# Pooled attention and a mixing block on one core: the softmax division moved behind the attention phase, and a new order of work inside it

## The chip, the cores and the metric

One core of one Trainium2 chip runs the whole program in one launch. The metric is the time of the device in microseconds (us), median of the runs. The engines are named as in the profile: PE (matrix multiply; PEld is its weight load), DVE (vector), ACT (scalar), POOL (GpSimd) and SP, whose queue issues nearly all DMAs.

## The reference

```python
# q, k, v: (8, 8, 1152, 64); the weights of the second part come in double precision (float64)
q_pool = q.reshape(B, H, S // 2, 2, D).mean(axis=3)
scores = scale * np.matmul(q_pool, k.transpose(0, 1, 3, 2))
scores = scores - np.max(scores, axis=-1, keepdims=True)
attn = np.exp(scores)
attn = attn / (np.sum(attn, axis=-1, keepdims=True) + 1e-09)
attn_out = np.matmul(attn, v)
x = attn_out.transpose(0, 2, 1, 3).reshape(B, 576, 512)

theta = x @ w_theta
zr, zi = x * np.cos(theta), x * np.sin(theta)
y = einsum('ts,bsd->btd', w_tok_r, zr) + einsum('ts,bsd->btd', w_tok_i, zi)
u = x + y
out = u + np.maximum(u @ w_ch, 0.0)
```

## The kernel before, in words

There are two phases. **Phase one** is the attention. It goes over 32 *pairs* (8 batches, 4 pairs of heads each; the two heads of a pair share the 128 partitions). Each pair has

- `prep`: PE transposes K and the pooled Q into a PSUM tile `pt` (`prep_t`, L240), in two groups; ACT rounds it to `hi` (`prep_hi`, L256), DVE takes the rest `lo` (`prep_lo`, L267), and ACT copies the last 64 queries of each head into `tail` (`prep_tail`, L263);
- the maxima: 12 products `pm` of Q blocks with K (`maxpass`, L280), each reduced by DVE (L287), and the `tail` products `px` and a corner of `pt` (`max_tail`, L297 and L303), reduced by DVE at L306 and L307. `max_nm` joins them to `nm`, `max_row` transposes `nm` on PE (L317) and ACT copies the row to `mT` (L319), and `load_max` spreads `mT` by four small DMAs into `nmr`, which the scores add as a fourth term;
- the scores, 18 units (u is the half of the queries, kt the block of keys): 8 matrix products `pe` (`escore`, L346), the exponential on ACT into `pc` (L349), and for 14 of the 18 a running sum `ss` on POOL (`ssum`, L358);
- `av`, twice: 36 recorded products `pa` of `pc` with V (L367), copied to `xu` by ACT (L374);
- the normalisation: `norm_sum` adds the sums over partitions on PE (L383), ACT adds epsilon into `sm` (L392). `norm_spread` writes `sm` to DRAM, `norm_load` reads it back over 128 partitions, DVE inverts it (L407), `norm_save` writes it, `norm_bcast` reads it with two DMAs as `dn` over all partitions, `norm_out` multiplies `xu` by `dn` on DVE (L429), and `norm_store` writes the result to `xd`.

The order is a table of positions. One unit of position is one score unit, so a pair is 18 long; `at(pos, ...)` collects every step, and all are emitted sorted by position. Every engine and SP's queue run in that order. `AV_AT` puts two *bursts* into a pair. Burst 0 (10.348) is `prep` group 1 of pair i+2, the maxima row of pair i+1, `av` 0, and `norm_sum` of pair i-1. Burst 1 (19.269) is `prep` group 0 of pair i+3, `max_tail` of pair i+2, and `av` 1. PSUM tiles of phase one (`bank2`) come from one ring of four double banks: whoever takes the next one waits until the user four places earlier is read out. K lies in one tile `kn`: its load for pair i+3 starts after burst 0 and must have landed for burst 1.

Between these steps lie the steps of `weights`, a generator that turns the double words of the weights into single precision and splits them (18 jobs: 8 square blocks, 10 token blocks). One call of it per position in `W_AT` does one step: a load, or one DVE, ACT or POOL operation (L500 to L530), or for a token block five transposes on PE (L565, L572) with their splits.

**Phase two** is the mixing block, one batch per 56 units of its own table (some 60 us): `xload` brings `xT` from `xd` into one of two buffers, ACT and the `xlo` engine split it (`xh` L700, `xl` L704), PE forms `theta` (`pth`, L724), `chain` makes sine and cosine factors on DVE and ACT and splits them, with the lower parts `Z` on POOL (L771), and PE multiplies them with the token weights (`py`, L796) and the channel weights (`pr`, L835).

Of the kernel before, what the change touches and what calls it, by code (L numbers as in the profile page):

```python
# [78 lines left out]
def pooled_attention_moe_kernel(  # L79
# [83 lines left out]
    with ExitStack() as p1:
# [128 lines left out]
        def max_tail(i, pt):  # L292
# [13 lines left out]
            nc.vector.tensor_reduce(mx[:, 8, 0:2], pm, AX.X, ALU.max)  # L306
# [7 lines left out]
        def max_row(i):  # L314
            st = state[i]
            px = bank2("e", f"pmt{i}")
            nc.tensor.transpose(out=px[0:KT, 0, 0:P], in_=st["nm"], identity=ident)  # L317
            mT = st["mT"] = sml.tile([KT, P], F32R, tag="mT", name=f"mT{i}")
            nc.scalar.copy(mT, px[0:KT, 0, 0:P])  # L319
            return px  # L320
# [39 lines left out]
        def av(i, u):  # L360
            st = state[i]
            if u == 0:
                st["xu"] = nrm.tile([P, 2, HALF], F32, tag="xu", name=f"xu{i}", bufs=3)
# [10 lines left out]
            nc.scalar.copy(st["xu"][:, u, :], pa[:, 0, 0:HALF])  # L374

# [18 lines left out]
        def norm_spread(i):  # L394
            st = state[i]
            rdi = st["rd"] = dram.tile([4, HALF], F32, tag="rd", name=f"rd{i}", bufs=2)
            nc.sync.dma_start(rdi, st["sm"].rearrange("(n r) c -> n r c", r=32)[:, 0, :])

        def norm_load(i):
            st = state[i]  # L400
            rc = st["rc"] = sml.tile([P, SQ * 2 // P], F32, tag="rc", name=f"rc{i}")
            rdv = st["rd"].rearrange("n c -> (n c)").rearrange("(p j) -> p j", p=P)
            nc.sync.dma_start(rc, rdv)

        def norm_recip(i):
            rc = state[i]["rc"]
            nc.vector.reciprocal(rc, rc)  # L407

        def norm_save(i):
            st = state[i]  # L410
            rdo = st["ro"] = dram.tile([4, HALF], F32, tag="ro", name=f"ro{i}", bufs=2)
# [4 lines left out]
        def norm_bcast(i):
            st = state[i]
            dn = st["dn"] = nrm.tile([P, 2, HALF], F32, tag="dn", name=f"dn{i}")
            for h in range(2):
                nc.sync.dma_start(  # L420
                    dn[h * D : (h + 1) * D].rearrange("a u c -> a (u c)"),
                    st["ro"].rearrange("(h u) c -> h (u c)", h=2)[h : h + 1, :].broadcast_to(
                        [D, SQ]
                    ),
                )

        def norm_out(i):
            st = state[i]
            nc.vector.tensor_tensor(st["xu"], st["xu"], st["dn"], ALU.mult)  # L429
# [33 lines left out]
        def norm_store(i):
# [5 lines left out]
            del state[i]  # L469

        def weights():
# [8 lines left out]
            def fetch(parts, n):  # L480
                ws = wst.tile([P, SQ], F32, tag="ws", name="ws")
                raw = wst.tile(
                    [P, SQ, 2 if wide else 1], U32 if wide else F32, tag="raw", name="raw"
# [3 lines left out]
                return raw, ws  # L487

            def narrow(raw, ws, R, n, g):
                dst = ws[0:R, 0:n].rearrange("a (t p) -> a p t", t=g)  # L490
                if not wide:
                    nc.vector.tensor_copy(
                        dst, raw[0:R, 0:n, 0].rearrange("a (p t) -> a p t", t=g)
                    )
                    return
# [7 lines left out]
                nc.vector.tensor_scalar(f, hi, 0x7FFFFFFF, None, ALU.bitwise_and)  # L503
# [455 lines left out]
```

## Time and profile before

| what | us |
|---|---|
| median of 3 runs (1422.18 to 1427.7) | 1422.18 |
| span of the profiled execution, first to last instruction | 1422.1 |
| start of `av` 0 of the first pair | 44.86 |
| start of `av` 0 of the 30th pair, 29 periods later | 857.53 |
| that stretch: PE busy / POOL busy | 768.15 / 697.91 |
| from 950 to 1400 (phase two in its stride): PE busy of 450 | 447.76 |

The profiled execution agrees with the median to 0.1 us, so nothing that matters lies around the span. "Busy" of PE includes waits inside a run of matrix products, since their ends are modelled. A row of the timeline reads: start, duration, engine, line and operation, what it writes from what, count, and in brackets how long the engine had been idle and what ended that. A row of the waits reads: who waited for whom, total time, how often, the longest. A row of the windows reads: stretch, its length, then busy time of PE, PEld, DVE, ACT and POOL with counts, the granted clock, the share of the DMA engines and GB/s. A row of the chain that ended last reads: start, duration, what.

### The profile page before, as it was taken

The page shows a single profiled execution, that of the slowest core. Times are in us where ns is not written, and L with a number is a line of the kernel's source. Part 1 is how long each engine was busy: PE and PEld are TensorE (multiplying, and loading weights), DVE is VectorE, ACT ScalarE, POOL GpSimd, SP SyncE. Part 2 cuts the span into 40 slices and gives each one's busy share as a digit, 9 for nine tenths or more (in the row PEclk, how much of TensorE's full clock was granted, in tenths as well). Part 3 has the DMA queues.
Part 4 walks back from the last instruction along what each step waited for, and adds up shares of the span by engine and source line. Part 5 has one row for each costly group of instructions (what it writes and reads, how often), then busy time and mean ns, then how long its engine had stood idle before and what let it go on. Part 6 is the DMA issues. An engine that isn't in the chain of part 4 may idle for free.

```text
span 1422.1 us, 29902 instructions
## 1 busy us (share of the span) xinstructions
PE 1343.2 (94%) x12178; PEld 1094.5 (77%) x12178; DVE 858.6 (60%) x1140; ACT 724.5 (51%) x1254; POOL 913.0 (64%) x671
## 2 busy tenths in 40 slices
PE   5999899999999999999998999989999999999998
PEld 4767677767766776767676776679999999999998
DVE  5866676667677767766675667165353543536342
ACT  2555455646555565556564655564344544445431
POOL 2789788988897998879987898842323313232210
PEclk9999999999999999999999999989999999999999
DMA  5224333424342353324333431321111111111111
GB/s 126 74 75 128 82 101 93 110 83 125 94 116 79 98 140 89 91 83 126 99 94 85 118 85 49 98 100 38 34 38 34 52 57 34 38 34 42 30 32 36
DMA packets 130906, 111.66 MB, mean 79 GB/s; under 512 B 95040, under 2 KB 95424, under 8 KB 130768
## 3 DMA queue, kind: packets, MB, share of 16 engines
q1 hardware_dynamic: 130592, 109.28, 28.0%
q8 instruction: 96, 1.57, 0.5%
q0 software_dynamic: 176, 0.46, 0.1%
q14 instruction: 42, 0.34, 0.1%
HBM read 88.29 MB, written 21.27 MB: 77 GB/s over the span
## 4 chain that ended last, share of the span: by engine, by line
PE 64%; DVE 18%; ACT 6%; DMA 5%; issue 3%; POOL 3%; SPq 1%; ACTq 0%; POOLq 0%; DVEq 0%
PE pe L346 15%; PE py L796 13%; PE pa L367 11%; PE pth L724 7%; DVE mx L287 6%; PE pr L835 6%; PE pm L280 3%; PE pt L240 3%; DMA kn<-in_k_dram 2%; PE pmt L383 2%; POOL ss L358 2%; DVE lo L267 2%; DVE ws L505 1%; DVE wf L503 1%; DVE mx L306 1%
## 5 line engine op out<-in xcount | busy, mean ns | idle before, releaser
L358 POOL TENSOR_TENSOR ss<-ss,pc 128x576 f32<-128x576 f32 x384 | 561.0, 1461 | 110.8 <-ACT pc L349 88.7
L287 DVE TENSOR_REDUCE mx<-pm 128x2 f32<-128x768 f32 x384 | 344.5, 952 | 138.2 <-PE pm L280 138.0
L349 ACT ACTIVATE pc<-pe 128x576 f32<-128x576 f32 x576 | 365.0, 652 | 90.0 <-PE pe L346 71.6
L367 PE MATMUL pa<-pc,vn 128*64 128x288 f32 x2304 | 293.5, 409 | 1.1 <-PE pmt L317 1.0
L771 POOL TENSOR_TENSOR Z<-ab,Z 128x512 fp32r<-128x512 f32 x40 | 52.3, 1308 | 315.1 <-ACT Z L767 315.1
L796 PE MATMUL py<-wtk,Z 128*128 128x288 f32 x1728 | 244.7, 299 | 6.9 <-DVE r L741 6.9
L367 PEld LDWEIGHTS pa<-pc,vn 128*64 128x64 f32 x2304 | 162.3, 137 | 109.5 <-ACT pc L349 3.2
L796 PEld LDWEIGHTS py<-wtk,Z 128*128 128x128 f32 x1728 | 235.7, 191 | 8.7 <-DVE r L741 7.5
L346 PE MATMUL pe<-hi 64*128 64x288 f32 x1152 | 206.4, 353 | 19.2 <-DVE lo L267 17.5
L346 PEld LDWEIGHTS pe<-hi 64*128 64x128 f32 x1152 | 110.6, 187 | 87.5 <-issue 28.8
L346 PE MATMUL pe<-lo,hi 64*128 64x288 f32 x1152 | 173.3, 296 | 0.0
L346 PE MATMUL pe<-hi,lo 64*128 64x288 f32 x1152 | 173.0, 295 | 0.0
L346 PE MATMUL pe<-nmr,oner 64*128 64x288 f32 x1152 | 172.3, 294 | 0.0
L280 PE MATMUL pm<-hi 64*128 64x384 f32 x768 | 138.2, 357 | 10.8 <-DVE mx L306 6.0
L256 ACT CAST hi<-pt 128x768 fp32r<-128x768 f32 x64 | 56.2, 878 | 117.8 <-DVE mx L307 103.1
L346 PEld LDWEIGHTS pe<-lo,hi 64*128 64x128 f32 x1152 | 112.1, 190 | 0.0
L346 PEld LDWEIGHTS pe<-hi,lo 64*128 64x128 f32 x1152 | 111.4, 189 | 0.0
L346 PEld LDWEIGHTS pe<-nmr,oner 64*128 64x128 f32 x1152 | 111.3, 188 | 0.0
L267 DVE TENSOR_TENSOR lo<-pt,hi 128x768 fp32r<-128x768 f32 x64 | 67.6, 1056 | 65.1 <-ACT hi L256 65.1
L835 PEld LDWEIGHTS pr<-us,wch 128*128 128x128 f32 x768 | 104.5, 188 | 1.8
L835 PE MATMUL pr<-us,wch 128*128 128x288 f32 x768 | 105.8, 295 | 0.0
L358 POOL TENSOR_TENSOR ss<-pc,pc 128x576 f32<-128x576 f32 x64 | 95.3, 1489 | 3.5 <-ACT pc L349 3.4
(103 smaller groups left out, 1653.7 us busy)
## 6 DMA issues: line engine op xcount, KB each, us to landing
qn<-in_q_dram SPq DMA_DIRECT2D x32, 576.0 KB
kn<-in_k_dram SPq DMA_DIRECT2D x64, 288.0 KB
vn<-in_v_dram SPq DMA_DIRECT2D x32, 576.0 KB
dn<-ro SPq DMA_DIRECT2D x64, 144.0 KB
xd<-xu SPq DMA_DIRECT2D x32, 288.0 KB
xT<-xd SPq DMA_DIRECT2D x8, 1152.0 KB
out_dram<-on SPq DMA_DIRECT2D x23, 192.0 KB
out_dram<-on SPq DMA_DIRECT2D x23, 128.0 KB
```

The source lines that it names most:

```text
L256: nc.scalar.copy(hi, src)
L267: nc.vector.tensor_tensor(lo, src, hi.bitcast(F32), ALU.subtract)
L280: nc.tensor.matmul(pm[:, h, 0:W], hi[hs, Q0 + j * P : Q0 + (j + 1) * P], hi[hs, K0[3 * g] : K0[3 * g] + W], start=True, stop=True,)
L287: nc.vector.tensor_reduce(mx[:, j : j + 5 : 4, g : g + 1], pm[:, :, 0:W], AX.X, ALU.max)
L346: nc.tensor.matmul(pe[:, h, 0:HALF], w[hs], x[hs], start=(n == 0), stop=(n == 3))
L349: nc.scalar.activation(pcs[u, kt], pe[:, :, 0:HALF], AF.Exp, scale=SC)
L358: nc.gpsimd.tensor_tensor(st["ss", u], first, st["pc"][u, kt], ALU.add)
L367: nc.tensor.matmul(pa[hs, 0, 0:HALF], st["vn"][:, h, kt, :], st["pc"][u, kt][:, h, :], start=(kt == 0), stop=(kt == KT - 1),)
L724: nc.tensor.matmul(th, xs[:, c, j * P : (j + 1) * P], ws[:, c], start=(n == 0), stop=(n == 11))
L771: engine("zlo", b).tensor_tensor(Z[1], t, Z[0].bitcast(F32), ALU.subtract)
L796: nc.tensor.matmul(st["py", c, u][:, 0:HALF], Z[zi][:, c * P : (c + 1) * P], wtk[wi][:, kw, u * HALF : (u + 1) * HALF], start=(i == 0 and ...
L835: nc.tensor.matmul(pr[u][:, 0:HALF], wch[wi][:, c, e * P : (e + 1) * P], st["us", ui][:, c, u * HALF : (u + 1) * HALF], start=(n == 0), st ...
```

## The change

The division leaves phase one. `norm_spread` writes the four sums of a pair into `sd` of its batch, and `norm_store` writes `xu` undivided as soon as `av` 1 is done (position 20.5 instead of 46.6). Per batch there is one load of all sums (`rload`), one reciprocal on DVE, one store (`rsave`); in phase two `dload` brings one 128-row block of factors (two DMAs), and `xscale` multiplies `xT` in place, two operations per block: on DVE for batch 0, on POOL for the others. `xload` of later batches moves from 64.6 units ahead of their base to 79.5.

The order of phase one is new. `max_tail` is cut in two: its products stay in place, its two reductions (`max_tail_red`) go behind `prep_hi`. The positions of the 12 maxima shift (`MAX_AT`). The maxima row is no longer made ahead of `av` 0 in a bank of its own but behind it, into the second half of the bank of `pa`; ACT copies `mT` after `xu`, and `norm_sum` takes a bank of its own. The steps of `weights` now have a kind (F load, A ACT, D DVE, G POOL, S rounding, T transposes) and run only at slots of their kind (`W_SLOTS`): two D slots lie directly behind each burst, T and A directly ahead of burst 0. A job takes one pair, so 18 jobs take the first 19 pairs. The raw words have two buffers. The DVE operations L500 (shift) and L503 (mask) go, and ACT gets an Abs beside its conversion.

```diff
-MAX_AT = (-24.792, -23.501, ..., -11.488, -10.057, -9.003)
+MAX_AT = (-24.5, -22.5, -21.5, -19.5, -18.5, -16.8, -15.5, -13.5, -12.5, -10.5, -9.5, -7.8)
-W_AT = (9.455, 9.493, 9.833, 9.896, 12.767, 17.992, 18.599, 19.246, 19.685)
+W_SLOTS = ((2.6, "F"), (3.0, "G"), (5.0, "G"), (5.5, "S"), (7.0, "G"), (10.345, "T"), (10.346, "A"), (10.36, "D"), (10.37, "D"), (12.6, "F"), (19.28, "D"), (19.29, "D"))
-    "max_nm": -8.851,
+    "max_nm": -7.66,
-    "norm_load": 29.426, ... "norm_out": 46.5, "norm_store": 46.6,
+    "norm_store": 20.5,
-PLAN2 = {'wload': 12.0, 'xload': -64.6, ...}
+PLAN2 = {'wload': 12.0, 'xload': -79.5, ...}
-X1_AT = -4
+R_AT = (16.0, 24.5, 24.6)
+DN_AT = (-83.9, -83.8, -83.7, -69.3)
+SC_AT = (-69.4, -69.3, -60.0, -59.9)
+    def dload(b, c):
+        dn = bst[b]["dn", c] = dnp.tile([P, SQ], F32, tag="dn", name=f"dn{b}_{c}", bufs=3)
+        for h in range(2):
+            src = rd[b].rearrange("(h u) c -> h (u c)", u=2)[2 * c + h : 2 * c + h + 1, :]
+            nc.sync.dma_start(dn[h * D : (h + 1) * D], src.broadcast_to([D, SQ]))
+    def xscale(b, c, eng):
+        xT, dn = bst[b]["xT"], bst[b]["dn", c]
+        eng.tensor_tensor(xT[:, c, 0:SQ], xT[:, c, 0:SQ], dn, ALU.mult)
+        eng.tensor_tensor(
+            xT[:, c, SQ : 5 * P], xT[:, c, SQ : 5 * P], dn[:, 4 * P : SQ], ALU.mult
+        )
         def av(i, u):
...
+            more = u == 0 and i + 1 < NPAIR
+            if more:
+                max_row(i + 1, pa)
             nc.scalar.copy(st["xu"][:, u, :], pa[:, 0, 0:HALF])
+            if more:
+                max_copy(i + 1, pa)
         def burst(i, u):
...
-                px = max_row(i + 1) if i + 1 < NPAIR else bank2("e", f"pmt{i}")
                 av(i, u)
                 if i > 0:
-                    norm_sum(i - 1, px)
+                    norm_sum(i - 1, bank2("e", f"pn{i}"))
         def tail_prep(i):
...
             if more:
                 prep_hi(i + 3, 0)
+            if i + 2 < NPAIR:
+                max_tail_red(i + 2)
+            if more:
                 prep_lo(i + 3, 0)
-                nc.vector.tensor_scalar(lo, lo, 8, None, ALU.logical_shift_right)
-                nc.vector.tensor_scalar(f, hi, 0x7FFFFFFF, None, ALU.bitwise_and)
+                nc.scalar.activation(mk, hi.bitcast(F32), AF.Abs)
+            for c in range(ND):
+                at(X0_AT + X0_DN[c], 13, dload, 0, c)
+                at(X0_AT + X0_SC[c], 14, xscale, 0, c, nc.vector)
```

What moves is seen in the engines' orders. First DVE at burst 1 in the middle of phase one, before (`ws`, `wf` and `raw` are tiles of the weights; `mx` collects the maxima):

```order
162 L503 TENSOR_SCALAR wf<-raw 128x576
163 L505 TENSOR_SCALAR ws<-wf 128x576
164 L507 TENSOR_SCALAR wf<-ws 128x576
165 L306 TENSOR_REDUCE mx_2469<-px_2609 128x2
166 L307 TENSOR_REDUCE mx_2469<-pt_8_2602 128x1
167 L267 TENSOR_TENSOR lo_2601<-pt_8_2602,hi_2600 128x768
168 L407 RECIPROCAL rc_2475<-rc_2475 128x9
169 L511 SCALAR_TENSOR_TENSOR wf<-raw,wf 128x576
```

and DVE at burst 1 with the change:

```order
180 L314 TENSOR_REDUCE mx_2877<-pm_12_2998 128x2
181 L338 TENSOR_REDUCE mx_2877<-px_3011 128x2
182 L339 TENSOR_REDUCE mx_2877<-pt_9_3004 128x1
183 L294 TENSOR_TENSOR lo_3003<-pt_9_3004,hi_3002 128x768
184 L524 SCALAR_TENSOR_TENSOR wf<-raw,wf 128x576
185 L528 TENSOR_SCALAR raw<-wf 128x576
```

Three steps of the weights stood ahead of the tail's reductions and of `lo`; now two stand behind `lo`, and none ahead. Second ACT at burst 0, before:

```order
177 L349 ACTIVATE pc_11_2772<-pe_11_2773 128x576
178 L256 CAST hi_2600<-pt_8_2784 128x960
179 L263 CAST tail_112<-pt_8_2784 64x64 x2
180 L319 CAST mT_2800<-pmt_2798 9x128
181 L374 COPY xu_2802<-pa_0_2803 128x288
182 L392 ACTIVATE sm_2831<-pmt_2798,eps 128x288
```

and ACT at burst 0 with the change:

```order
189 L385 ACTIVATE pc_11_2784<-pe_11_2785 128x576
190 L514 ACTIVATE ws<-raw 128x576
191 L515 ACTIVATE raw<-raw 128x576
192 L283 CAST hi_2615<-pt_8_2804 128x960
193 L290 CAST tail_131<-pt_8_2804 64x64 x2
194 L413 COPY xu_2818<-pa_0_2819 128x288
195 L351 CAST mT_2840<-pa_0_2819 9x128
196 L433 ACTIVATE sm_2851<-pn_2842,eps 128x288
```

`mT` went from ahead of `xu` to behind it, and two operations of the weights went ahead of `hi`. Third SP's queue behind burst 0, before (the last of the four loads of `nmr` first):

```order
90 L327 DMA nmr_109<-mT_2800 1x16x4
91 L466 DMA xd_83<-xu_2020 128x576
92 L201 DMA kn_2839<-in_k_dram 128x9x64 x2
93 L215 DMA vn_2853<-in_v_dram 128x2x576
94 L397 DMA rd_2855<-sm_2831 4x288
95 L403 DMA rc_2863<-rd_2855 128x9
96 L412 DMA ro_3032<-rc_2863 128x9
97 L486 DMA raw<-in_moe_w_theta_dram 128x1024
98 L420 DMA dn_3037<-ro_3032 64x576 x2
```

and SP's queue behind burst 0 with the change:

```order
94 L363 DMA nmr_127<-mT_3231 1x16x4
95 L228 DMA kn_3250<-in_k_dram 128x9x64 x2
96 L242 DMA vn_3264<-in_v_dram 128x2x576
97 L437 DMA sd_91<-sm_3242 4x288
98 L497 DMA raw<-in_moe_w_theta_dram 128x1024
99 L479 DMA xd_83<-xu_3209 128x576
100 L218 DMA qn_3551<-in_q_dram 96x2x768
```

The K load still stands behind the four `nmr` loads, which need `mT`; the store of `xd` between them moved behind `vn`, and three kinds of small transfers and the two of `dn` are gone from the pair.

More of the change, by code (lines that the diff above doesn't have):

```diff
@@ L129, in pooled_attention_moe_kernel @@
     xd = [dram.tile([DM, SQ], F32, name=f"xd{b}") for b in range(B)]
+    sd = [dram.tile([2 * H, HALF], F32, name=f"sd{b}") for b in range(B)]
+    rd = [dram.tile([2 * H, HALF], F32, name=f"rd{b}") for b in range(B)]
+    dnp = ctx.enter_context(tc.tile_pool(name="dnp", bufs=1))
     def bank(kind, name):
@@ L312, in max_nm, with max_row, max_copy, first_row @@
             nc.vector.tensor_reduce(nm, st["mx"], AX.X, ALU.max, negate=True)
[L314 to L320, printed above, removed]
+        def max_row(i, px):
+            nc.tensor.transpose(out=px[0:KT, 1, 0:P], in_=state[i]["nm"], identity=ident)
+        def max_copy(i, px):
+            mT = state[i]["mT"] = sml.tile([KT, P], F32R, tag="mT", name=f"mT{i}")
+            nc.scalar.copy(mT, px[0:KT, 1, 0:P])
+        def first_row():
+            px = bank2("e", "pmt0")
+            max_row(0, px)
+            max_copy(0, px)
         def load_max(i):
@@ L394, in norm_spread @@
         def norm_spread(i):
[L395 to L411, printed above, removed]
+            b, hp = divmod(i, NP)
             nc.sync.dma_start(
-                rdo.rearrange("n c -> (n c)").rearrange("(p j) -> p j", p=P), st["rc"]
+                sd[b][4 * hp : 4 * hp + 4], state[i]["sm"].rearrange("(n r) c -> n r c", r=32)[:, 0, :]
             )
[L416 to L429, printed above, removed]
+            del state[i]
         def burst(i, u):
@@ L480, in fetch @@
             def fetch(parts, n):
-                ws = wst.tile([P, SQ], F32, tag="ws", name="ws")
                 raw = wst.tile(
-                    [P, SQ, 2 if wide else 1], U32 if wide else F32, tag="raw", name="raw"
+                    [P, SQ, 2 if wide else 1], U32 if wide else F32, tag="raw", name="raw", bufs=2
                 )
@@ L494, in narrow @@
                     )
+                    yield "F"
                     return
@@ L584, in token, with wstep @@
                     split(dst[0], dst[1], src, nc.scalar, nc.vector)
-                yield
-            jobs = []
+            groups = []
             for w, dst in ((w_theta, wth), (w_ch, None)):
                 wv = words(w).rearrange("(c p) e o -> p c e o", p=P)
-                jobs.append([square(wv, c, dst) for c in range(ND)])
+                groups.append([(square, wv, c, dst) for c in range(ND)])
             for w, kb in ((w_tok_r, 0), (w_tok_i, 4)):
                 wv = words(w).rearrange("(p t) s o -> t p s o", t=QT)
-                jobs.append([token(wv, kb, jt) for jt in range(5)])
-            for n in range(5):
-                for group in jobs:
-                    if n < len(group):
-                        yield from group[n]
+                groups.append([(token, wv, kb, jt) for jt in range(5)])
+            jobs = [g[n] for n in range(5) for g in groups if n < len(g)]
+            yield "F"
+            coming = jobs[0][0](*jobs[0][1:])
+            for n in range(len(jobs)):
+                now = coming
+                for kind in now:
+                    if kind == "F":
+                        yield "F"
+                        if n + 1 < len(jobs):
+                            fn, *args = jobs[n + 1]
+                            coming = fn(*args)
+                    else:
+                        yield kind
+        def wstep(kinds):
+            if wkind[0] and wkind[0] in kinds:
+                wkind[0] = next(wgen, None)
         def early():
-            run(wgen)
+            while wkind[0]:
+                wstep(wkind[0])
             pw.close()
@@ L661, in pooled_attention_moe_kernel @@
         wgen = weights()
+        wkind = [next(wgen)]
+        for b in range(B - 1):
+            for n, fn in enumerate((rload, recip, rsave)):
+                at(NU * (4 * b + 4) + R_AT[n], 12, fn, b)
         at(X0_AT, 11, early)
+        for c in range(ND):
+            at(X0_AT + X0_DN[c], 13, dload, 0, c)
+            at(X0_AT + X0_SC[c], 14, xscale, 0, c, nc.vector)
         for i in range(NPAIR):
-            for pos in W_FIRST if i == 0 else W_AT if i < W_END else W_LAST:
-                at(NU * i + pos, 10, next, wgen, None)
+            for pos, kinds in W_SLOTS:
+                at(NU * i + pos, 10, wstep, kinds)
         for _, _, _, fn, args in sorted(todo, key=lambda e: e[:3]):
@@ L893, in pooled_attention_moe_kernel @@
             if b > 0:
-                at2(base + PLAN2["xload"] if b > 1 else X1_AT, xload, b)
+                if b == B - 1:
+                    for n, fn in enumerate((rload, recip, rsave)):
+                        at2(-60 + 10 * n, fn, b)
+                at2(base + PLAN2["xload"], xload, b)
+                for c in range(ND):
+                    at2(base + DN_AT[c], dload, b, c)
+                    at2(base + SC_AT[c], xscale, b, c, nc.gpsimd)
             xat = PLAN2["xhi"] if b else THETA0_AT[0] - 4
```

97 lines of the change are left out of this document (47 added, 50 removed).

## The prediction

> **What bounds the kernel now.** I read the busy times first, then stretches by stage, then PE's waits in the stage that is changed, then single pairs in the timeline and in the chain that ended last.
>
> ```profile
> PE 1343.2 (94%) x12178; PEld 1094.5 (77%) x12178; DVE 858.6 (60%) x1140; ACT 724.5 (51%) x1254; POOL 913.0 (64%) x671
> ```
>
> PE carries the program; POOL is the next, far behind on the whole. The windows say where.
>
> ```profile
> 44.86:857.53 812.67, 768.15 (x8034) 571.15 (x8034) 566.96 (x669) 453.95 (x795) 697.91 (x505) 0.99 0.37 98
> ...
> 950.00:1400.00 450.00, 447.76 (x3082) 426.00 (x3082) 203.66 (x353) 199.38 (x336) 131.07 (x94) 1.00 0.13 37
> ```
>
> Phase two in its stride leaves PE idle 2.2 us of 450: nothing to win there. What can move is the first row, 29 periods of a pair, 812.67/29 = 28.02 each, where PE idles 44.5. PE's waits in it:
>
> ```profile
> PE pe L346 <- DVE lo L267: 17.5, 12, 1.6
> PE pmt L383 <- ACT mT L319: 11.5, 9, 2.4
> PE pm L280 <- DVE mx L306: 6.0, 4, 2.6
> PE pt L240 <- DMA kn<-in_k_dram: 5.6, 7, 1.2
> ```
>
> How long is a period without them? One such pair, PE and ACT:
>
> ```profile
> 634.89 4.59 PE L367 MATMUL pa<-pc,vn 128*64 128x288 f32 x36
> 647.15 0.87 PE L240 MATMUL pt<-ident,kn 128*128 128x128 f32 x6
> 660.70 0.71 PE L367 MATMUL pa<-pc,vn 128*64 128x288 f32 x4
> ...
> 637.08 0.42 ACT L263 CAST tail<-pt 64x64 fp32r<-64x64 f32 x2 [1.23 <-DVE lo L267]
> 637.53 0.26 ACT L319 CAST mT<-pmt 9x128 fp32r<-9x128 f32 x1
> 639.53 0.40 ACT L374 COPY xu<-pa 128x288 f32<-128x288 f32 x1 [1.75 <-PE pa L367]
> ```
>
> From `av` 0 to the next pair's `av` 0 it is 660.70 - 634.89 = 25.81 us. Burst 1's transposes start 647.15 - 639.48 = 7.67 after `av` 0's end; `mT` was done 1.7 before that end. So 812.67 - 29 x 25.81 = 64 us of phase one are losses.
>
> **The change, part by part.** *Weight steps behind bursts, rounding ahead of tail maxima.* A pair that lost:
>
> ```profile
> 340.12 2.22 DVE L503 TENSOR_SCALAR wf<-raw 128x576 uint32<-128x576 uint32 x1
> 342.45 1.48 DVE L505 TENSOR_SCALAR ws<-wf 128x576 f32<-128x576 f32 x1
> 343.84 1.21 DVE L306 TENSOR_REDUCE mx<-px 128x2 f32<-128x1024 f32 x1
> 347.13 0.40 PE L346 MATMUL pe<-hi 64*128 64x288 f32 x2 [1.41 <-DVE lo L267]
> ```
>
> Two weight steps held the tail's reductions, these held `hi` (ACT, next in order), `hi` held `lo`, and PE wanted `pt`'s bank back. In the new order of DVE nothing of the weights stands ahead of burst 1's reductions, and `hi` runs beside them, so `lo` is done some 1.21 + 0.3 (L307, an eighth as wide) + 1.16 at most (a row below) = 2.7 after the tail's products, and the two steps behind it (1 to 1.5 each by the rows above, alone) end at about the end of `av` 1 (4.59). The 17.5 and 6.0 go. The half clock that followed the longest of these stalls goes with them:
>
> ```profile
> 289.00:297.00 8.00, 6.14 (x60) 5.77 (x60) 5.85 (x10) 5.42 (x9) 5.32 (x5) 0.79 0.26 70
> ```
>
> A clock of 0.79 over 8 us is 1.7 us lost, after two stalls. I name no further sum for it, since I count by periods.
>
> *The maxima row behind `av` 0.* The 11.5 go too (`norm_sum` no longer shares `mT`'s bank). But `mT` now always comes after `av` 0, and the K load stands behind it in SP's queue. What that means shows in a pair in which `mT` was late because of weight steps; chain, SP's queue, PE:
>
> ```profile
> 302.14 1.16 DVE lo L267
> ...
> 303.78 0.26 ACT mT L319
> ...
> 307.99 4.92 DMA kn<-in_k_dram
> ```
>
> ```profile
> 304.06 0.66 SPq L326 DMA_DIRECT2D nmr<-mT  x1
> ...
> 306.66 0.57 SPq L466 DMA_DIRECT2D xd<-xu  x1
> 307.33 1.51 SPq L201 DMA_DIRECT2D kn<-in_k_dram  x2
> ```
>
> ```profile
> 299.43 4.59 PE L367 MATMUL pa<-pc,vn 128*64 128x288 f32 x36
> ...
> 313.05 0.84 PE L240 MATMUL pt<-ident,kn 128*128 128x128 f32 x6 [1.15 <-DMA kn<-in_k_dram]
> ```
>
> `mT` ended at 304.04, as `av` 0 did (304.02); the K load was issued 3.29 later, the first 2.60 for four `nmr` loads; it was in 5.72 after that, and PE idled 1.15. With the change: `mT` ends after `av` 0, one transposition (0.84/6, say 0.15), `xu` 0.40 and `mT` 0.26, together about 0.85. SP then needs 3.29 less the moved store (307.33 - 306.66 = 0.67), 2.62. The load takes 5.72, or where it was fastest 0.66 + 4.35 + 0.14 = 5.15:
>
> ```profile
> 784.29 4.35 DMA kn<-in_k_dram
> ```
>
> So burst 1 can start 8.6 to 9.2 after `av` 0's end, where PE would be ready at 7.67 + 0.15. That is an idle time of 0.8 to 1.4 in each of 29 pairs, where now 7 pairs wait 5.6 in all. I take 1.05, the middle. Queued behind this wait on SP are V, the sums and the next weights, all wanted later. So this part turns a wait that some pairs had into one that all have: 25.81 + 1.05 = 26.86 a period.
>
> *Token transposes* (T) move to one place, ahead of burst 0, in 10 pairs:
>
> ```profile
> 184.59 0.66 PE L565 MATMUL pwt<-ident,ws 128*128 128x128 f32 x4
> 186.01 0.71 PE L240 MATMUL pt<-ident,qp 96*128 96x96 f32 x6
> ```
>
> From 184.59 to 186.01 is 1.42 where 0.2 would do: 1.2 each, 12 in all.
>
> *Sum of the 29 periods:* 29 x 26.86 + 12 = 791, against 812.7: 21.7 less.
>
> *The division.* Per pair it takes two small loads and a store, two broadcast loads, a reciprocal and a multiplication off SP and DVE:
>
> ```profile
> L429 DVE TENSOR_TENSOR xu<-xu,dn 128x576 f32<-128x576 f32 x32 | 35.7, 1117 | 12.8 <-DMA dn<-ro 12.8
> ```
>
> These 35.7 us lay beside `av` and score products in 30 pairs: nothing on the path. The removed DVE steps L500 and L503 and ACT's new Abs are as idle. Of the new steps, batch 0's eight multiplications (4 x 1.1 and a little) run on DVE in the last pair, which has no maxima left; the cover is that pair, and without it they would cost 5. For batches 1 to 7 POOL multiplies, per batch 4 x 1.46 by `ss`'s row below and four short ones, some 7 us beside a POOL that is busy 131 of 450: free in the stride, since `xT` is loaded when the batch two before is added. At the start of phase two it is not:
>
> ```profile
> 928.60 0.43 DVE L744 TENSOR_SCALAR r<-r 128x512 f32<-128x512 f32 x1
> 936.48 1.41 DVE L744 TENSOR_SCALAR r<-r 128x512 f32<-128x512 f32 x1
> 946.43 1.81 PE L796 MATMUL py<-wtk,Z 128*128 128x288 f32 x6 [4.53 <-DVE r L741]
> ...
> 955.13 6.14 POOL L704 TENSOR_TENSOR xl<-xT,xh 128x640 fp32r<-128x640 f32 x4
> ```
>
> ```profile
> 946.43 16.41 PE py L796 x105
> ```
>
> POOL starts batch 1's `xl` behind its last `Z` at 955.13 and ends it at 961.3; with the 7 us of `xscale` among these `Z`, less the idle time POOL has there, `xl` may end near 967. How much of these 6 us reaches PE, none of these rows shows: 0 if PE still has enough of `py` to do (the chain's row: batch 0's first half of `py` runs from 946.43 for 16.4), 6 if not. I take +2, since that half ends at 962.8, in between. DVE drops one `norm_out` there (0.7 at best, since PE waits for DVE's `r`). Together +1.3, with ends of -0.7 and +6.
>
> Sum: -21.7 + 1.3 = -20.4 against the profiled execution's 1422.1, which is the median's 1422.18: **1402**.
>
> **A rule of the skill against a row.** DVE's same operation took 0.43 alone and 1.41 while POOL ran (rows above). The Trainium skill, "SBUF — State Buffer", Who interferes with whom, says that DVE and GpSimd share one port pair under an exclusive lock, and that the loser waits for the whole instruction. The trace agrees. By the rule POOL would lose some of the time of the DVE steps that now stand beside its sums, and of the masks that it waits for, and the time would be that of the third rival, 1420 to 1429; by the sum above it is 1402.
>
> **The rivals.** *First: K lands almost in time.* If the load takes 0.5 less than the fastest row shown, the stall is 0.3 instead of 1.05: 29 x 0.75 = 22 less, 1380. The even spacing of the maxima, which could shorten the other half by tenths, has the same effect. Against it: both loads shown took over 5 us until PE started, and the pair has hardly fewer bytes to move.
>
> *Second, slower: `mT` later still.* On ACT two weight operations now stand ahead of `hi`, `lo`, `tail`, `xu`, `mT`.
>
> ```profile
> L256 ACT CAST hi<-pt 128x960 fp32r<-128x960 f32 x32 | 30.6, 956 | 4.9 <-PE pt L240 4.9
> ```
>
> By this row, 512 or 576 columns take some 0.7, so both 1.4; with `hi` 0.96, `lo` 1.16 and two `tail` 0.42 it is 3.9 against `av` 0's 4.59. If ACT enters the burst late by two exponentials (1.3), `mT` is 0.7 late, in T pairs 2; each us passes through SP to PE. From 0.75 us per pair on (21.7/29) the gain is gone; at 1.5 in all pairs it is 1402 + 44 = 1446, at 2.0 in the 18 weight pairs 1438.
>
> *Third: POOL becomes the bound.*
>
> ```profile
> L358 POOL TENSOR_TENSOR ss<-ss,pc 128x576 f32<-128x576 f32 x384 | 561.0, 1461 | 110.8 <-ACT pc L349 88.7
> L209 POOL TENSOR_TENSOR qp<-qn 96x384 f32<-96x384 f32 x62 | 64.1, 1053 | 22.6 <-PE pt L240 15.3 <-DMA qn<-in_q_dram 7.3
> L519 POOL TENSOR_TENSOR ws<-wf,raw 128x512 f32<-128x512 f32 (+2 forms) x18 | 24.8, 1378 | 0.7
> L517 POOL TENSOR_TENSOR raw<-raw 128x512 f32<-128x512 f32 (+2 forms) x18 | 19.8, 1097 | 11.2 <-DVE raw L515 11.2
> ```
>
> A whole job per pair in the first 18: 14 x 1.46 + 2 x 1.05 + 1.10 + 1.38 = 25.0, in square pairs one more of about 1.3, 26.3 of 26.86. If waits for DVE's masks and DVE's lock add 2 per pair there, 18 x 1 to 1.5 come back: 1420 to 1429.
>
> *Fourth: the clock.* A stall in every pair might halve the clock each time, 1.7 us by the row above: 1402 + 29 x 1.7 = 1451. The Trainium skill, "TensorE: Matmul & The Clock Gate", A second HAM failure mode, tells of such an oscillation from frequent short idling. The pair shown with 1.15 idle had no half clock, so I give it little.
>
> *Fifth: the stalls on `lo` stay* since something else holds DVE: 1402 + 17 = 1419.
>
> **How the numbers follow.** Forecast 1402: 0.54. First rival 0.14. Third and fifth, in full or in part, 1412 to 1429: 0.19. Second: 0.10. Fourth: 0.03. A measurement here tells about 0.5% (7 us) from no change, so faster means under 1415: 0.54 + 0.14 + 0.05 of the third and fifth = 0.73; same 0.15; slower 0.12. The range 1377 to 1423 leaves out the slower rivals and little of the first; the likeliest case alone has 1394 to 1412 (0.8 and 1.4 for the stall).
>
> **What would show it.** In the new trace PE's waits for `lo`, `mT` and L306's counterpart should be near nothing, and the wait of `pt` for `kn` should be the largest in phase one, about 29 times 1; `mT` should end 0.8 to 1 after each `av` 0; the period should be near 26.9 (28 with T); POOL's busy share in the first 18 pairs should be over 93%; `xl` of batch 1 should end near 967 less the 20 won. I am wrong if K lands before 7.8, if `mT` lies beyond 1.5, or if exponentials wait for POOL.

## The result, and the profile after

The changed kernel takes 1399.72 us (median of 4 runs, 1399.06 to 1400.52), the kernel before 1422.51 beside it: a ratio of 0.9836, with a 95% interval of 0.9815 to 0.9858. The forecast was 1402. Its profiled span is 1397.3 against 1422.1. Where the 24.8 went, by the starts of the same work in both traces (`uT` is the first addition of a batch on DVE, L812 before and L836 now):

| stretch | before | after | difference |
|---|---|---|---|
| to `av` 0 of pair 0 | 44.86 | 44.57 | -0.3 |
| 29 periods of phase one | 812.67 | 777.35 | -35.3 |
| the two pairs behind them | 46.36 | 44.21 | -2.2 |
| `av` 0 of the last pair to the end of PE's wait at `pend` | 16.43 | 19.62 | +3.2 |
| to `uT` of batch 0 | 41.63 | 45.08 | +3.4 |
| to `uT` of batch 1 | 60.77 | 64.06 | +3.3 |
| to `uT` of batch 7, six batches | 362.51 | 366.18 | +3.7 |
| to the end | 36.88 | 36.23 | -0.6 |

So phase one gave 37.8, and everything behind it took 13.0 back. The busy times and two windows of the changed kernel (same columns as before):

```profile
PE 1324.2 (95%) x12178; PEld 1081.9 (77%) x12178; DVE 817.3 (58%) x1056; ACT 726.4 (52%) x1272; POOL 957.4 (69%) x727
```

```profile
44.57:821.92 777.35, 745.70 (x8039) 557.51 (x8038) 519.92 (x591) 457.55 (x817) 687.21 (x506) 1.00 0.34 93
...
1000.00:1380.00 380.00, 375.36 (x2586) 355.73 (x2585) 179.35 (x304) 166.31 (x280) 142.84 (x114) 1.00 0.17 51
```

In phase one PE idles 31.7 of 777.35, where it was 44.5 of 812.67. The rest of the 35.3 lies inside "busy" time. Part of it is the clock, 0.99 over this stretch before and 1.00 now: the trace of before has 17.1 us at half clock there (6.8 from 149 on, and 3.4 each from 292, 582 and 767), which cost some 8.5, half of it, and the changed kernel's has none. In the stride of phase two it idles 4.6 of 380, where it was 2.2 of 450. PE's waits in those 29 periods:

```profile
PE pt L267 <- DMA kn<-in_k_dram: 25.4, 24, 2.7
PE pt L267 <- DVE mx L314: 4.1, 4, 1.1
PE pt L267 <- issue: 0.6, 1, 0.6
```

The waits for `lo` and `mT` are gone. These rows are one wait: `pt` of burst 1, in all 29 pairs, for K. In five of them the last semaphore seen was another one, but the load landed just ahead of `pt` there too. Together 30.1, or 1.04 a pair. One pair shows how:

```profile
609.98 4.59 PE L403 MATMUL pa<-pc,vn 128*64 128x288 f32 x36
614.50 0.28 PE L347 MATMUL pa<-ident,nm 128*9 128x128 f32 x1
...
615.11 0.25 ACT L351 CAST mT<-pa 9x128 fp32r<-9x128 f32 x1
615.38 0.65 SPq L362 DMA_DIRECT2D nmr<-mT  x1
...
618.05 1.39 SPq L228 DMA_DIRECT2D kn<-in_k_dram  x2
...
623.00 0.85 PE L267 MATMUL pt<-ident,kn 128*128 128x128 f32 x6 [0.69 <-DMA kn<-in_k_dram]
```

`mT` ends at 615.36, 0.79 after `av` 0 (614.57), and 0.79 or 0.80 in 28 of the 29 pairs. SP then issues four `nmr` loads until 617.95 and K at 618.05; PE can start on it 4.95 later.

Behind phase one PE waits for these:

```profile
PE py L820 <- DVE r L765: 6.9, 2, 4.7
PE pend L424 <- POOL ss L394: 4.9, 1, 4.9
PE po L882 <- ACT on L899: 4.8, 7, 0.8
PE pth L748 <- POOL xl L728: 2.3, 2, 1.3
```

The first is as before. The other three stood at 1.7, 1.5 and nothing before. The second is the last pair's sums. In the timeline, DVE's `xscale` of batch 0 beside them:

```profile
874.35 11.35 POOL L394 TENSOR_TENSOR ss<-ss,pc 128x576 f32<-128x576 f32 x6
874.95 1.44 DVE L179 TENSOR_TENSOR xT<-xT,dn 128x64 f32<-128x64 f32 x1
...
885.75 0.70 PE L424 MATMUL pend<-ss,ones 128*32 128x288 f32 x3 [4.88 <-POOL ss L394]
```

and the same six sums before:

```profile
911.44 8.83 POOL L358 TENSOR_TENSOR ss<-ss,pc 128x576 f32<-128x576 f32 x6
```

They took 2.5 longer. The sum just ahead of them, beside `xscale` too, took 1.94 instead of 1.42. The third comes once per batch, from `xscale` of a later batch on POOL:

```profile
1041.95 1.43 POOL L178 TENSOR_TENSOR xT<-xT,dn 128x576 f32<-128x576 f32 x1
1043.01 0.92 DVE L785 TENSOR_TENSOR ab<-xn,ab 128x512 f32<-128x512 f32 x1 [1.85 <-ACT ab L782]
1043.96 0.62 ACT L791 CAST Z<-ab 128x512 fp32r<-128x512 f32 x1 [1.40 <-DVE ab L785]
1044.49 0.58 ACT L899 COPY on<-po 128x512 f32<-128x512 f32 x1
1045.12 0.66 PE L882 MATMUL po<-ident,uT 128*128 128x128 f32 x4 [0.77 <-ACT on L899]
```

At the same place before:

```profile
1069.59 0.63 ACT L758 ACTIVATE ab<-r 64x512 f32<-64x512 f32 x1
1070.32 0.69 DVE L761 TENSOR_TENSOR ab<-xn,ab 128x512 f32<-128x512 f32 x1 [1.50 <-ACT ab L758]
...
1072.21 0.66 PE L858 MATMUL po<-ident,uT 128*128 128x128 f32 x4 [0.17 <-ACT on L875]
```

DVE's product starts 0.45 after ACT's `ab` (ended 1042.56) instead of 0.10, and takes 0.92 instead of 0.69; `Z`, `on` and `po` follow it, and PE idles 0.77 instead of 0.17.

### The profile page after: what moved, and what is told of

Same layout as the page of the kernel before. It is cut to its first block, busy times and chain, and to the rows that moved or that the text cites. A ratio compares the mean times of both kernels' runs of the same rounds, so it can differ in the third digit from the quotient of the medians.

```text
span 1397.3 us, 29769 instructions
## 1 busy us (share of the span) xinstructions
PE 1324.2 (95%) x12178; PEld 1081.9 (77%) x12178; DVE 817.3 (58%) x1056; ACT 726.4 (52%) x1272; POOL 957.4 (69%) x727
## 4 chain that ended last, share of the span: by engine, by line
PE 76%; DMA 9%; DVE 5%; ACT 4%; issue 2%; POOL 2%; SPq 1%; POOLq 0%; ACTq 0%; DVEq 0%
PE pa L403 20%; PE pe L382 17%; PE py L820 12%; DMA kn<-in_k_dram 8%; PE pth L748 7%; PE pr L859 6%; PE pt L267 4%; PE pm L307 3%; PE pn L424 2%; DVE mx L314 2%; PE pxn L736 1%; PE px L324 1%; POOL ss L394 1%; ACT pc L385 1%; ACT xh L724 1%
## 5 line engine op out<-in xcount | busy, mean ns | idle before, releaser
L394 POOL TENSOR_TENSOR ss<-ss,pc 128x576 f32<-128x576 f32 x384 | 552.9, 1440 | 85.7 <-ACT pc L385 61.5
L314 DVE TENSOR_REDUCE mx<-pm 128x2 f32<-128x768 f32 x384 | 355.5, 956 | 182.3 <-PE pm L307 181.7
L385 ACT ACTIVATE pc<-pe 128x576 f32<-128x576 f32 x576 | 353.9, 652 | 63.3 <-PE pe L382 42.8
L403 PEld LDWEIGHTS pa<-pc,vn 128*64 128x64 f32 x2304 | 159.5, 137 | 109.5 <-issue 3.3
L382 PE MATMUL pe<-hi 64*128 64x288 f32 x1152 | 198.1, 340 | 1.8 <-DVE mx L314 0.7
L382 PE MATMUL pe<-lo,hi 64*128 64x288 f32 x1152 | 170.4, 292 | 0.0
L382 PE MATMUL pe<-hi,lo 64*128 64x288 f32 x1152 | 170.2, 292 | 0.0
L307 PE MATMUL pm<-hi 64*128 64x384 f32 x768 | 134.1, 347 | 3.9 <-ACT hi L283 2.1
L413 ACT COPY xu<-pa 128x288 f32<-128x288 f32 x64 | 25.6, 400 | 166.9 <-PE pa L403 123.9
L382 PEld LDWEIGHTS pe<-lo,hi 64*128 64x128 f32 x1152 | 109.1, 186 | 0.0
```

Source lines behind the costliest of these rows:

```text
L307: nc.tensor.matmul(pm[:, h, 0:W], hi[hs, Q0 + j * P : Q0 + (j + 1) * P], hi[hs, K0[3 * g] : K0[3 * g] + W], start=True, stop=True,)
L314: nc.vector.tensor_reduce(mx[:, j : j + 5 : 4, g : g + 1], pm[:, :, 0:W], AX.X, ALU.max)
L382: nc.tensor.matmul(pe[:, h, 0:HALF], w[hs], x[hs], start=(n == 0), stop=(n == 3))
L385: nc.scalar.activation(pcs[u, kt], pe[:, :, 0:HALF], AF.Exp, scale=SC)
L394: nc.gpsimd.tensor_tensor(st["ss", u], first, st["pc"][u, kt], ALU.add)
L403: nc.tensor.matmul(pa[hs, 0, 0:HALF], st["vn"][:, h, kt, :], st["pc"][u, kt][:, h, :], start=(kt == 0), stop=(kt == KT - 1),)
```

## Experiments

The kernel before took 1422 to 1426 beside these runs, so kernels are compared by their ratios to it, and places by their own traces.

**K load first.**

```diff
-    "load_k": -43.209,
+    "load_k": -43.645,
```

> The changed kernel with the K load of pair i+3 put ahead of the four nmr loads in SP's queue (position 10.355 instead of 10.791); nothing else. Theory: the 30 us that PE waited for kn in 29 pairs are there because the load is issued behind mT. Issued right after burst 0's transpositions it lands about 5.5 after av 0's start, 1 after its end, long before burst 1: the waits for kn go to under 3 in all, a period from 26.8 to 25.8, total about 1370. Rival 1: POOL, which was busy 24.6 to 26.5 per pair in the 18 weight pairs, takes over there, so that only the pairs behind them gain: about 1385. Rival 2: nmr now lands late behind the bigger load and PE waits for it instead: about 1400.

1378.17 us, ratio 0.9675 (0.9653 to 0.9696). The waits for `kn` are gone, all of them; a period without weight steps is 25.50. The gain is 22, not 30. Behind av 0 of pair 0, which comes 2.9 later (K of pair 2 now stands ahead of the first `nmr` loads), the 29 periods fell by 24.9, so 5 of the 30.1 came back, in the pairs with weights. Windows of the 17 pairs with weights and the 11 behind them:

```profile
72.12:518.96 446.84, 440.85 (x4744) 329.47 (x4743) 352.61 (x382) 281.37 (x502) 431.39 (x314) 1.00 0.39 105
518.96:799.94 280.98, 280.73 (x3037) 209.59 (x3036) 163.50 (x191) 162.12 (x287) 241.78 (x179) 1.00 0.31 81
```

POOL (the fifth of the busy times) is busy 431.39 of 446.84 in the first, 97%. PE's largest wait is now this one:

```profile
PE pm L307 <- ACT pc L385: 4.1, 7, 0.8
```

A product waits for a PSUM bank that the exponential on ACT has still to read. All seven lie in pairs of square jobs, and ahead of each one ACT waited for POOL, to round the weights:

```profile
199.74 0.62 ACT L541 CAST hl<-ws 128x512 fp32r<-128x512 f32 x1 [0.86 <-POOL ws L532]
```

Both answers hold a part: the load's place explains the wait, and POOL is next in the pairs with square jobs.

**The row back ahead of `av` 0.**

```diff
-            more = u == 0 and i + 1 < NPAIR
-            if more:
-                max_row(i + 1, pa)
...
-            if more:
-                max_copy(i + 1, pa)
...
+                px = bank2("e", f"pmt{i}")
+                if i + 1 < NPAIR:
+                    max_row(i + 1, px)
+                    max_copy(i + 1, px)
                 av(i, u)
                 if i > 0:
-                    norm_sum(i - 1, bank2("e", f"pn{i}"))
+                    norm_sum(i - 1, px)
```

> The maxima row back ahead of av 0, in a bank of its own that norm_sum shares, mT ahead of xu on ACT; the rest as in the changed kernel. If it is only the row's place behind av 0 that makes kn late, then mT is done some 3 us earlier, the kn waits (30 us) go, and the total is about 1372. Rival: the last maxima and nm now stand directly ahead of burst 0, so PE waits for nm on DVE in every pair instead (reduction 1.2 + nm 0.3, less the transpositions 0.9: 0.6 to 1.2 each, 17 to 35 in all): 1387 to 1405, and the move behind av 0 was right only for these positions.

1385.31 us, ratio 0.9722 (0.9701 to 0.9744); the 29 periods take 763.02.

```profile
PE pmt L347 <- DVE nm L344: 7.4, 19, 0.4
PE pt L267 <- DMA kn<-in_k_dram: 4.2, 7, 1.3
PE pmt L419 <- ACT mT L351: 3.1, 8, 0.6
```

The wait for K falls from 30.1 to 4.2, and 10.5 come as new waits for `nm` and `mT`. Both mechanisms are there; the row's move behind `av` 0, with K behind it in SP's queue, costs 14 by itself.

**Reductions ahead of rounding.**

```diff
-            if more:
-                prep_hi(i + 3, 0)
-            if i + 2 < NPAIR:
                 max_tail_red(i + 2)
             if more:
+                prep_hi(i + 3, 0)
                 prep_lo(i + 3, 0)
```

> The tail's two reductions back ahead of the rounding hi of burst 1 (hi then waits for DVE again); the rest as in the changed kernel. Theory: with no weight step ahead of the reductions hi and lo come about 0.9 later, which the bank ring still covers: 1400 to 1403. Rival: PE needs that bank back sooner, and pays 0.5 to 0.9 in each pair: 1414 to 1426.

1407.29 us, ratio 0.988 (0.985 to 0.9911). The 29 periods take 782.40. The changed kernel and three others here that have the same program up to that point took 777.35, 779.16, 780.44 and 781.76, so the rival's 14 to 26 are excluded. The median lies between the two forecasts, and whether this part is worth anything at all isn't settled. No wait for `lo` came back.

**Weight steps ahead of the bursts.** First the D slots alone:

```diff
-... (10.36, "D"), (10.37, "D"), (12.6, "F"), (19.28, "D"), (19.29, "D"))
+... (9.5, "D"), (9.9, "D"), (12.6, "F"), (18.0, "D"), (18.6, "D"))
```

> The four weight steps on DVE put ahead of the bursts again (positions 9.5, 9.9, 18.0, 18.6 instead of 10.36, 10.37, 19.28, 19.29); the rest as in the changed kernel. Theory: they hold reductions and lo as in the kernel before, so PE waits for lo or the maxima 1 to 1.5 per weight pair: 18 to 27 more, less what the kn wait would have cost anyway: 1410 to 1425. Rival: with the operations L500 and L503 gone and hi ahead of the reductions, DVE catches up in time: 1400.

1428.28 us, ratio 1.0026 (1.0008 to 1.0044), but not for the reason in question. The two D steps need the A step, whose slot at 10.346 now stands behind theirs, so a job took two pairs, and what was left of the weights was done in one go near the end. The waits from 860 to 900:

```profile
PE pwt L574 <- POOL ws L532: 19.7, 3, 7.4
```

This run doesn't tell what the steps cost while a job takes one pair. So again, with T and A moved along:

```diff
-... (10.345, "T"), (10.346, "A"), (10.36, "D"), (10.37, "D"), (12.6, "F"), (19.28, "D"), (19.29, "D"))
+... (9.3, "T"), (9.4, "A"), (9.5, "D"), (9.9, "D"), (12.6, "F"), (18.0, "D"), (18.6, "D"))
```

> The changed kernel with all weight steps of a burst ahead of it: T, A and the two D at 9.3, 9.4, 9.5, 9.9, the other two D at 18.0 and 18.6, so that a job still takes one pair. Theory: DVE's order has two weight steps ahead of the tail's reductions and of nm again, lo comes up to 2.9 later, PE waits for lo or the maxima 1 to 1.5 in each weight pair, behind the kn wait and not in its shade: 18 to 27 more than the changed kernel's 1400, 1418 to 1427. Rival: there is slack on DVE by now and PE's waits there stay under 0.3 a pair: 1400 to 1405.

1422.16 us, ratio 0.9979 (0.9958 to 0.9999): the size that the theory gave, the whole gain of the change lost. The 29 periods of the profiled execution, one of the longer ones (1427.38), take 805.94, 28.6 more. The place is another one:

```profile
PE pt L267 <- DMA kn<-in_k_dram: 38.3, 26, 3.0
PE pt L267 <- DVE raw L528: 3.9, 2, 2.0
...
PE pt L267 <- DVE mx L314: 1.1, 1, 1.1
```

PE has no wait for `lo`; ACT has. At burst 0 of one pair:

```profile
249.52 0.42 ACT L290 CAST tail<-pt 64x64 fp32r<-64x64 f32 x2 [3.15 <-DVE lo L294]
```

The steps ahead of the burst hold `lo` on DVE, `tail` on ACT waits for `lo`, and `xu` and `mT` come behind `tail`. So `mT` ends up to 1.0 later than in the changed kernel, and K behind it: 43.3 of waiting for K instead of 30.1, 13 more. Most of the rest is the clock. After an idle time of 2.23 a window of 5 us:

```profile
146.50:151.50 5.00, 4.93 (x28) 3.38 (x30) 2.96 (x4) 0.80 (x1) 4.92 (x5) 0.66 0.40 158
```

Half clock came in six places, 24 us in all, half of which, some 12, I count as lost.

**The old positions of the maxima.**

```diff
-MAX_AT = (-24.5, -22.5, ..., -10.5, -9.5, -7.8)
+MAX_AT = (-24.792, -23.501, ..., -11.488, -10.057, -9.003)
```

> The changed kernel with the 12 maxima of a pair at the positions they had before (MAX_AT alone). Theory: the even spacing is what made the second half of a pair (burst 1 to burst 0) 0.3 shorter, since a product no longer waits for a PSUM bank that DVE reads: the periods grow by 0.3 in all 29 pairs, 9 in all: about 1409. Rival: that half is shorter because DVE's weight steps and norm_out are gone from it, and the positions don't matter: 1400.

1408.57 us, ratio 0.9882 (0.9861 to 0.9903). A second half (`av` 1 to the next `av` 0) behind the weights, changed kernel, then this one:

```profile
598.08 4.59 PE L403 MATMUL pa<-pc,vn 128*64 128x288 f32 x36
609.98 0.71 PE L403 MATMUL pa<-pc,vn 128*64 128x288 f32 x4
```

```profile
601.87 4.59 PE L403 MATMUL pa<-pc,vn 128*64 128x288 f32 x36
614.00 0.71 PE L403 MATMUL pa<-pc,vn 128*64 128x288 f32 x4
```

11.90 against 12.13: 0.23 here, and 0.20 a pair on the mean of the 29, 6 in all. So the positions do count, at two thirds of the size that the theory gave. Its mechanism, the wait for a PSUM bank, is not shown: PE has no idle time in either of these halves, and the 0.2 lies inside its runs of score products.

**The division alone**, on the kernel before: the division's hunks, none of the order.

```diff
-    "norm_load": 29.426, ... "norm_store": 46.6,
+    "norm_store": 20.5,
... (sd, rd, rload, recip, rsave, dload, xscale and their positions as in the change)
```

> The kernel before with the division moved alone (sums to sd, undivided store at 20.5, dload and xscale in phase two, xload at -79.5); the order of phase one and the weight steps as before. Theory: the 35.7 us of multiplications and the loads lay beside PE, so phase one keeps its 28.0 a period within 0.3, while the start of phase two loses what the changed kernel lost there (about 13: POOL's sums beside xscale 3, a half clock 3, xl of batch 1 late 3.4, one wait of 0.6 per batch 4): 1428 to 1436. Rival: without norm_out on DVE and the eight DMAs per pair on SP, kn and lo come earlier and phase one falls by 0.5 a period or more: 1408 to 1422.

1426.85 us, ratio 1.0017 (1.0004 to 1.0031), between the two forecasts. In phase one it won 9.9, in part by the rival's mechanism; from `av` 0 of the last pair to the end it took 530.1 where it was 518.2, 11.9 more.

```profile
44.08:846.89 802.81, 765.01 (x8034) 567.70 (x8034) 538.29 (x621) 453.27 (x795) 688.63 (x505) 0.99 0.33 90
```

```profile
PE pe L376 <- DVE lo L297: 16.8, 12, 1.6
PE pmt L413 <- ACT mT L349: 15.2, 11, 2.8
PE pt L270 <- DMA kn<-in_k_dram: 1.9, 3, 1.2
```

The waits for `kn` and for the tail's reductions shrank by 3.7 and 5.1; those for `lo` stayed, and those for `mT` grew by 3.7. Some 3.4 of the 9.9 is the clock, 10.2 us at half clock here against 17.1 before, and such windows differ between executions of one program (last section). So of the 35.3 of phase one the division gave 9.9 and, by difference of single profiles, everything else that is new in phase one 25.4; and the division lost its part behind.

**The last pair's sums.**

```diff
-            nc.gpsimd.tensor_tensor(st["ss", u], first, st["pc"][u, kt], ALU.add)
+            eng = nc.vector if i == NPAIR - 1 and u == 1 else nc.gpsimd
+            eng.tensor_tensor(st["ss", u], first, st["pc"][u, kt], ALU.add)
-X0_SC = (5.0, 5.5, 6.0, 9.0)
+X0_SC = (5.0, 5.5, 6.0, 13.0)
```

> The changed kernel with the last pair's second set of running sums on DVE instead of POOL (and batch 0's fourth xscale behind them); nothing else. Theory: PE's 4.9 at pend is POOL's sums, slowed by xscale on DVE, and the half clock of 10 us behind it follows from that idle time. DVE ends these sums near 880.5, when av 1 ends: the 4.9 go, the half clock at 883 goes, another 2 to 3: 1391 to 1393. Rival: DVE, with five multiplications and seven sums in a row, is itself late, and xl of batch 0 behind it: 1396 to 1400.

1396.18 us, ratio 0.9801 (0.9768 to 0.9834). By the totals alone that isn't apart from the changed kernel; by the trace, `av` 0 of the last pair to the end takes 524.0 instead of 531.2, 7.2 less.

```profile
876.47 5.07 DVE L395 TENSOR_TENSOR ss<-ss,pc 128x576 f32<-128x576 f32 x6
...
881.25 0.79 PE L425 MATMUL pend<-ss,ones 128*32 128x288 f32 x5
881.46 0.75 DVE L178 TENSOR_TENSOR xT<-xT,dn 128x576 f32<-128x576 f32 x1
...
882.13 0.22 DVE L179 TENSOR_TENSOR xT<-xT,dn 128x64 f32<-128x64 f32 x1
```

`pend` waits for nothing (no bracket). The clock in the changed kernel, then in this one:

```profile
883.00:894.00 11.00, 7.59 (x30) 5.04 (x31) 3.00 (x3) 1.74 (x3) 2.61 (x2) 0.53 0.01 2
```

```profile
871.00:887.00 16.00, 15.29 (x149) 10.08 (x146) 12.87 (x19) 8.11 (x15) 2.93 (x2) 1.00 0.18 57
```

Here no half clock comes before 902.

**`xscale` early, and `xl` of batch 1 on DVE.**

```diff
-SC_AT = (-69.4, -69.3, -60.0, -59.9)
+SC_AT = (-69.4, -69.3, -69.2, -69.1)
```

> The changed kernel with xscale of blocks 2 and 3 of each later batch directly behind blocks 0 and 1 on POOL (SC_AT -69.2 and -69.1 instead of -60 and -59.9). Theory: the 0.77 that PE waits at po once per batch comes from POOL's xscale, which holds DVE's product for Z, which holds ACT's Z and the copy of po behind it; with POOL idle there the wait falls to 0.17 as before: 6 to 7 times 0.6, 4 less: 1395 to 1396. Rival: the same two multiplications stand now beside another chain step and cost the same there, or the fourth block's factors land late and hold POOL's Z: 1399 to 1403.

1402.16 us, ratio 0.9844 (0.9827 to 0.9861), no change. The waits, 4.8 in the changed kernel, went as expected:

```profile
PE po L882 <- ACT on L899: 1.7, 7, 0.5
```

but a batch fell by only 0.38 (61.18 to 60.80; before the change it was 60.47), in the four intervals from batch 2 to 6, 1.5 in all, and a third half clock of phase two, 3.4 us long, came at 940. The runs with K first and with the old positions have one there too without this edit, so it need not come from it.

```diff
-            engine("xlo", b).tensor_tensor(
+            (nc.vector if b == 1 else engine("xlo", b)).tensor_tensor(
```

> The changed kernel with batch 1's xl on DVE, which is idle from 921 to 931, instead of POOL; nothing else. Theory: PE's two waits for xl (1.3 and 1.0) go, and the first stream of py is as long as before (19.5 to the next instead of 22.9): 1396.5 to 1397.5. Rival: xscale of batch 1 on POOL ends only at 928.5, so xh and with it xl of the last block stay late by 1 or more, or DVE's uT slips behind them: 1399 to 1400.

1401.99 us, ratio 0.9837 (0.9822 to 0.9851). The mechanism holds: batch 0's `uT` to batch 1's takes 61.1 instead of 64.1. The total doesn't show it, since the 29 periods took 781.76 in this profile; from `av` 0 of the last pair to the end it won 1.8.

**All together**, with one step more: the last step of the square weight jobs goes from POOL to DVE.

```diff
-                eng.tensor_tensor(lo, src, hi.bitcast(F32), ALU.subtract)
+                nc.vector.tensor_tensor(lo, src, hi.bitcast(F32), ALU.subtract)
```

> The changed kernel with the K load ahead of the nmr loads, the last pair's second sums on DVE, batch 1's xl on DVE, xscale of blocks 2 and 3 early, and the last step of the eight square weight jobs (the lower part, POOL, 1.3) on DVE. Theory: the gains lie at different places and add up: 22.5 + 7 + 2 + 1, and if it is POOL that makes the square pairs 0.65 longer (26.68 instead of 26.03) than the token pairs once K is in time, 8 x 0.65 = 5 more: 1400 - 37 = 1363. Rival: the square pairs are long for another reason (DVE's weight steps), so that the step on DVE brings nothing or costs 0.7 each: 1368 to 1374.

1367.15 us, ratio 0.9593 (0.9573 to 0.9613). The square pairs, two in a row, fell from 26.69 and 26.67 to 26.51 and 26.07, and the waits of `pm` behind ACT's rounding are gone, so POOL it was, in part; the 29 periods won 2.8 on the K load alone. Token pairs take 26.05 and pairs without weights 25.49, so a token job costs 0.56 (from its first transposition to PE's next work it is 0.60). What is missing stands at the start of phase two:

```profile
898.65 5.34 PE L821 MATMUL py<-wtk,Z 128*128 128x288 f32 x28 [3.16 <-POOL Z L796]
```

The early `xscale` of batch 1 runs on POOL ahead of batch 0's last `Z`. Last, early only from the third batch on:

```diff
-                    at2(base + SC_AT[c], xscale, b, c, nc.gpsimd)
+                    at2(base + SC_AT[c] - (0 if b == 1 or c < 2 else 9.2), xscale, b, c, nc.gpsimd)
```

(with `SC_AT` as in the changed kernel)

> The best kernel so far with xscale early for the batches from the third on alone; batch 1's third and fourth stand behind batch 0's Z again, as in the changed kernel. Theory: in the kernel before this one PE idled 3.16 in the first stream of py, since POOL did these two multiplications ahead of batch 0's last Z; with Z first the 3.16 go, and the xl of batch 1, on DVE, ends some 2 after the last xscale, before PE wants it: 1364. Rival: xl of batch 1 is then late by 1 to 3 instead, as much as was won: 1366 to 1367.

**1362.72 us, ratio 0.956 (0.9541 to 0.9579)**: 37 less than the changed kernel by the medians, the fastest here. PE idles 1.9 of the 29 periods:

```profile
47.97:797.70 749.73, 747.80 (x8040) 557.79 (x8039) 535.71 (x599) 458.37 (x817) 683.36 (x498) 1.00 0.36 96
```

## Why the prediction was right, and where it was not

The new wait, the term on which the forecast turned, was right. That the total came out only 2 off is luck in part: three other terms were mis-sized, and the third gave back what the first two had won.

- *The new wait* was right in mechanism and size: `mT` 0.79 after `av` 0 (0.85 forecast), every pair waits, 1.04 on average (1.05 taken). The K load's place proves it: with it ahead, the waits are gone.
- *The waits for `lo`, `mT` and L306* went as forecast. That the new order, with its new weight steps, does it as a whole is shown by the run of the division alone, where PE still waits 16.8 and 15.2 for the first two. Which piece of it ends the waits for `lo` stays open: with the weight steps ahead of the bursts again, and with the reductions ahead of `hi` again, PE waits for `lo` in neither run, nor when K comes early. The two pieces may each be enough, or the two DVE operations that went; no run here parts them. What the place of the weight steps (with T and A) is worth is shown, 22, but by another way than the prediction's: through `lo`, `tail` and `mT` to the K load, and through half clocks.
- *The base of 25.81 a period* was mis-sized. Without waits it is 25.50, with the row's transposition in it: 9.0 less in 29 periods. It was read from a pair with the old spacing of the maxima, and some 0.2 of the 0.31 is that spacing. The prediction named this ("could shorten the other half by tenths") and counted it to a rival only.
- *T at 1.2 each, 12 in all*: what came on top of base and K wait is 777.35 - 29 x 25.50 - 30.1 = 7.75, and T is 0.56, at most 5.6 in ten pairs. Some 2 more lie in the 8 square pairs, whose second half is 0.26 longer than that of pairs without weights (12.16 against 11.90); why is not shown. These two terms, 9.0 and 4.3, make phase one 13 of the 14 better than the 791 forecast.
- *"Nothing on the path" for the division in phase one* was wrong in the kernel before (9.9, by the run of the division alone, some 3.4 of it clock).
- *What lies behind phase one, +1.3 with ends of -0.7 and +6*, failed: +13.0. The priced part, `xl` of batch 1, was near: it ended 21.5 after the stream of `py` began (20.6 forecast) and cost 3.3 (2 taken). Left out were batch 0's `xscale`, costed at nothing with the last pair as its cover: on DVE it was covered, but it slowed POOL's sums, for which PE waits (+3.2, and +3.4 with the half clock behind). And "free in the stride" was false: 0.71 a batch, but for the last. In both the wrong step was to look only at whether the engine that does the work is idle, not at its neighbour.
- *The weighed rule*: the Trainium skill, "SBUF — State Buffer", Who interferes with whom (a DVE instruction with two SBUF inputs and a GpSimd instruction that reads SBUF contend for one port pair, which the first one holds for its whole instruction). I let it bear on phase one, as a rival; what it tells of showed in the stretch behind. The trace agrees: 64 columns took DVE 1.44 beside POOL's sums and 0.22 without.
- *Rivals*: K almost in time did not happen; `mT` later still did not; POOL as the bound was hidden by the K wait, and with that gone it cost 4.1, in the square pairs alone; the clock stayed at 1.00 over the 29 periods of this profile, though not of every one (last section); no wait for `lo` was left.

## What to carry to other kernels

Where a load is queued behind something that is known late, its place in the queue is a price per round: moving one line here was worth as much as the whole change. When work goes to an idle engine, ask which engine runs slower beside it (here POOL beside DVE) and who waits for that one; a cover that hides the time of an operation doesn't hide this. And when a wait is removed, look for the busy share that it was hiding: POOL was at 93% of the weight pairs with the K wait in and at 97% without, and then ACT and PE waited for it in the square pairs.

## What the runs showed of the hardware that I had not expected

The same program had half-clock windows in some runs and not in others. Phase one of the changed kernel, of `last_sums_dve`, `scale_early` and `xl_one_dve` is the same up to the last pair, and their profiles have 0, 1, 1 and 2 such windows of 3.41 us in those 29 periods. Each came right after PE had waited 1.86 to 2.21 for K; a wait of 2.74 in the changed kernel left the clock at full speed, and so did waits of 1.81 to 2.71 in the other three. One of them, in `xl_one_dve`:

```profile
410.00:413.50 3.50, 3.50 (x18) 2.07 (x18) 2.52 (x4) 0.80 (x1) 3.31 (x3) 0.51 0.26 67
```

One and the same stretch takes 777.35 to 781.76 by this: about 1.7 for each window, estimated as half its length, and in two of the four profiles some 1.5 more of waiting for K. That is more than some of the edits above were worth. The Trainium skill, "TensorE: Matmul & The Clock Gate", HAM oscillation, warns of idle gaps over about 3.4 us; here gaps of 2 were enough at times. Part 1 of that page of the Trainium skill says that the window of observation runs freely. That would fit that it looks like chance here; no run shows the window itself.
